# Windowed attention with sinks, then a capacity-limited expert layer: half values by DMA, wider masks, scores two steps ahead

## The chip, the cores and the metric

The kernel runs on one core of a Trainium2 chip. The metric is the device time of one execution in microseconds, lower is better. Its engines are named as in the profile: PE (TensorE matmuls, with PEld for the weight loads), DVE (VectorE), ACT (ScalarE), POOL (GpSimd) and SP (SyncE, which here only issues DMAs). Each engine takes its instructions in the order in which the program issued them.

## What is computed

Four batches of eight heads, 768 positions, 64 elements a head. Attention sees the last 128 positions and the first four ("sinks"):

```
scores = scale * q @ k.T
keep   = (pos_k < 4) | ((rel >= 0) & (rel < 128))
a      = softmax(where(keep, scores, -1e9));  x = a @ v     # heads side by side: x is (4, 768, 512)
```

Then, for each batch, the 128 rows of x with the highest x @ w_gate go through an expert and are written over:

```
h  = relu(x[top] @ w1);  ye = h @ w2
out[top] = x[top] + sigmoid(score) * ye            # all other rows: out = x
```

## The kernel before, in words

**Steps.** The loop (line 380) runs over 24 steps: batch b, head group g (four heads), and jp, a pair of 128-row blocks of queries. Within a batch the six steps are numbered s = 3g + jp. Every engine's order is the order of the calls in this loop (`manual_schedule`, line 59); waits between engines follow from the tiles they share.

**Scores (line 188).** For each of e = 0, 1 (two heads each) PE multiplies a block of 128 keys with up to 256 queries into a PSUM tile `sc`, then the four sink keys against the halves of the blocks that need them. ACT takes exp of each `sc` (line 214) into a tile `pt`, one for each e. The exps need no maximum, since the scores are small.

**Masks (lines 218 to 232).** POOL sets to zero what lies outside the window, in place in `pt`: for each e four selections, on 64 partitions each, of 256 elements (128 for a part of jp = 2, where the last block has no successor), and at jp = 0 a memset of the four sink rows, where the sinks are ordinary keys. That is eight selections a step.

**Values (line 234).** For each e PE multiplies the masked weights with values, 16 products (12 at jp = 0), each recorded as two matmul instructions, into a PSUM tile `xg`. A column of ones behind the 64 values gives the sum of the weights; DVE takes its reciprocal and scales (lines 253, 254) into the tile `X` of the batch. There are two `xg`. The products use the full values `vb`, or one of two half tiles: `vlo` has the values of the lower 64 keys of each block and the sink values in rows from 64 on, `vhi` the values of the upper 64 and the sink values in rows from 0 on. So a product of 128 rows covers 64 window keys and the sinks.

**Where the half values come from.** The rest of `vlo` and `vhi` is zero (memsets on DVE, lines 140 to 143). SP writes the four sink rows from a tile `vst` (line 113). POOL copies the halves from `vb` (line 118), 64x512 elements at a time, two copies in each step, three steps ahead of use: group 1 of a batch during its steps 0 to 2, group 0 of the next batch during steps 3 to 5; the first group in the head.

**Transposes (line 163).** Queries and keys come by POOL's DMAs (line 84) into `kb` and `qb`, and PE turns them in groups of twelve into PSUM tiles `trp`, of which there are two (tag "w"); ACT and DVE copy one half each into `KT` and `QT`. For the next head group, keys are turned at jp = 0 and queries at jp = 1. `sink_keys` copies the sink columns.

**Expert layer (class Moe).** It runs one batch behind, in pieces put into the steps: scores spread and counted (s = 0, 1), rank and selection matrix (s = 2), row indices (s = 3), a gather of the chosen rows by an indirect DMA on POOL (s = 4, line 329), their transposition and the first product (s = 5); the second product and the scatter on POOL (line 365) follow in steps 0 to 2 of the batch after. The last batch's layer is the tail behind the loop.

**Head.** POOL issues eight loads of the first q and k in halves, then makes the identity matrix for the transposes (line 131), which DVE casts (line 133). DVE then clears the half tiles. All transposes of the first group stand ahead of the first scores (lines 372 to 377), and each step's scores are issued one step ahead of its values (line 386).

Of the kernel before, what the change touches and what calls it, by code (L numbers as in the profile page):

```python
# [15 lines left out]
B = 4  # L16
# [9 lines left out]
VS = 96  # L26
# [4 lines left out]
def kernel(  # L31
# [19 lines left out]
    pp = ctx.enter_context(tc.tile_pool(name="pp", bufs=6))  # L51
# [9 lines left out]
    def const(shape, dt, name):  # L61
        return cp.tile(shape, dt, name=name, tag=name)

    vb = [const([128, H, NB, VS], FP32, f"vb{i}") for i in range(2)]
# [53 lines left out]
    def copy_half_values(b, g, c0, c1):  # L118
        for dst, r in ((vlo, 0), (vhi, 64)):
            POOL.tensor_copy(out=dst[g][r:r + 64, :, c0:c1, 0:D], in_=vb[b % 2][r:r + 64, 4 * g:4 * g + 4, c0:c1, 0:D])  # L120
# [6 lines left out]
    DVE.memset(ident_f[:], 0.0)  # L127
    DVE.memset(vb[0][:, :, :, D:VW], 1.0)
    DVE.memset(ksk[0][:], 0.0)
    DVE.memset(ksk[1][:], 0.0)  # L130
    POOL.affine_select(out=ident_f[:], in_=ident_f[:], compare_op=ALU.not_equal, fill=1.0, base=0,
                       pattern=[[-1, 128]], channel_multiplier=1)
    DVE.tensor_copy(out=ident_b[:], in_=ident_f[:])  # L133
    load_qk(0, 1)
    DVE.memset(vst[:, :, :, D:VW], 1.0)
    for g in range(2):
        ACTE.copy(out=vst[:, 4 * g:4 * g + 4, :, 0:D],
                  in_=vsk[:, 4 * g:4 * g + 4, :].unsqueeze(2).to_broadcast((NSINK * B, 4, NB, D)))
    for g in range(2):
        DVE.memset(vlo[g][64:128, :, :, :], 0.0)  # L140
# [3 lines left out]
        load_sink_values(0, g)  # L144
        if g == 0:
            for jp in range(3):
                copy_half_values(0, 0, 2 * jp, 2 * jp + 2)
# [40 lines left out]
    def scores(b, g, jp):  # L188
# [11 lines left out]
        for e in range(2):  # L200
            qh = qt[:, e, :].rearrange("p (c m n) -> p c m n", m=2, n=64)
            last = 1 if jp == 2 else 2
            for l in range(2):
# [5 lines left out]
                          start=True, stop=True, skip_group_check=True)  # L209
        for e in range(2):  # L210
            pt = pp.tile([128, 2, 2, 256], FP32, name="pt", tag="pt")
            PT[(b, g, jp, e)] = pt
            if jp < 2:
                ACTE.activation(out=pt[:, :, :, :], in_=sc[e][:, :, :, :], func=ACT.Exp, scale=0.125)  # L214
            else:
                ACTE.activation(out=pt[:, :, 0, :], in_=sc[e][:, :, 0, :], func=ACT.Exp, scale=0.125)
                ACTE.activation(out=pt[:, :, 1, 0:128], in_=sc[e][:, :, 1, 0:128], func=ACT.Exp, scale=0.125)
            for r in (0, 64):
                o = pt[r:r + 64, :, :, r:r + 64].rearrange("p l c n -> p (l c) n")
                POOL.affine_select(out=o, in_=o, compare_op=ALU.is_ge, fill=0.0,  # L220
                                   base=0, pattern=[[0, 4], [1, 64]], channel_multiplier=-1)
            for r in (0, 64):
                if jp < 2:
                    o = pt[r:r + 64, :, :, 128 + r:192 + r].rearrange("p l c n -> p (l c) n")
                    n = 4
                else:
                    o = pt[r:r + 64, :, 0, 128 + r:192 + r]
                    n = 2
                POOL.affine_select(out=o, in_=o, compare_op=ALU.is_ge, fill=0.0,  # L229
                                   base=-1, pattern=[[0, n], [-1, 64]], channel_multiplier=1)  # L230
            if jp == 0:
                POOL.memset(pt[0:NSINK, :, 0, :].rearrange("p l (w n) -> p l w n", w=2)[:, :, :, 0:64], 0.0)  # L232

    def values(b, g, jp, t):
        xg = x_ps.tile([128, 2, 2, VW], FP32, name="xg", tag="xg")
        full = vb[b % 2][:, 4 * g:4 * g + 4, :, :]
        for i in range(2):
            j = 2 * jp + i
            new = PT[(b, g, jp, t)]
            old, o = (PT[(b, g, jp, t)], 0) if i else (PT.get((b, g, jp - 1, t)), 1)  # L240
            for l in range(2):
                hh = 2 * l + t
                terms = []
                if j:
                    terms.append((old[:, l, o, 128:192], full[:, hh, j - 1, 0:VW], 0))
                    terms.append((old[:, l, o, 192:256], vhi[g][:, hh, j - 1, :], 1))
                terms.append((new[:, l, i, 0:64], vlo[g][:, hh, j, :], 0))
                terms.append((new[:, l, i, 64:128], full[:, hh, j, 0:VW], 1))
# [123 lines left out]
    for t in range(2):  # L372
        transposes(0, 0, t, (0,))
    for t in range(2):
        transposes(0, 0, t, (1,))
    sink_keys(0, 0)
    scores(0, 0, 0)

    moe = {}
    for n, (b, g, jp) in enumerate(steps):  # L380
# [24 lines left out]
        if nxt[0] < B and jp == 0:  # L405
            transposes(nxt[0], nxt[1], 0)
# [94 lines left out]
```

## Time and profile before

| | us |
|---|---|
| median of 3 runs | 207.34 (206.05 to 207.49) |
| the profiled execution | 206.85 |
| its span in the trace | 205.1 |

The span is what the trace covers; the rest of the execution's time lies around it. In the stage tables each row is a stretch of the span: its length, the busy time of each engine with its count of instructions, the clock that PE was granted, the mean share of the sixteen DMA engines and GB/s. A line of a group reads: line, engine, operation, tiles written and read, shape, count, then busy us and mean ns of one, then the idle time before such instructions and what ended it. A line of the waits reads: who waited for whom, us in total, times, longest.

Two things about the numbers. PE's busy time includes the drain at the end of each burst of matmuls, so it is more than the time in which PE issues. And DMA shares can exceed 1, since packets of several queues overlap.

### The profile page before, as it was taken

The numbers are of one execution on the slowest core, as the hardware profiler recorded it, in microseconds if no ns is written. First come the engines' busy times: TensorE is split into PE (matmuls) and PEld (weight loads), VectorE is DVE, ScalarE is ACT, GpSimd is POOL, SyncE is SP. The second block draws the span as 40 slices with busy tenths as digits, with TensorE's granted clock in tenths as the row PEclk, the third lists the DMA queues.
The fourth block names the chain that finished last, engine by engine and source line by source line (L and its number), as shares of the span: only waits on it lengthen the run. The fifth ranks groups of instructions, "written<-read, shape, count | busy, mean of one in ns | idle before, by whom it ended". The sixth has DMA issues, their size and how long they took to land. (4 is left out here: it accounts for less than half of the span.)

```text
span 205.1 us, 5901 instructions
## 1 busy us (share of the span) xinstructions
PE 134.0 (65%) x2476; PEld 108.3 (53%) x2480; DVE 95.2 (46%) x286; ACT 74.4 (36%) x108; POOL 141.3 (69%) x295
## 2 busy tenths in 40 slices
PE   0317887598488929952999670780699945949470
PEld 0303775585387717841797460660587734837440
DVE  0581374186437725670078650353049751572610
ACT  0805454163316331430474542030265543332030
POOL 7933898988989889883798880784778785800111
PEclk9999999769859985695599998596589985666996
DMA  5999927087392999948508149024000012240111
GB/s 83 219 178 216 288 46 136 5 137 225 114 275 51 198 190 195 232 173 261 152 0 148 21 74 234 4 105 158 6 3 3 3 52 105 104 153 3 51 51 53
DMA packets 21786, 24.14 MB, mean 118 GB/s; under 512 B 7232, under 2 KB 17472, under 8 KB 21760
## 3 DMA queue, kind: packets, MB, share of 16 engines
q0 software_dynamic: 7168, 10.49, 28.2%
q1 hardware_dynamic: 14592, 13.28, 22.0%
q8 instruction: 19, 0.31, 0.6%
q14 instruction: 7, 0.06, 0.1%
HBM read 24.41 MB, written 7.34 MB: 155 GB/s over the span
## 5 line engine op out<-in xcount | busy, mean ns | idle before, releaser
L250 PE MATMUL xg<-vb,pt 128*64 128x65 f32 x704 | 62.6, 254 | 10.5 <-POOL pt L220 9.4
L250 PE MATMUL xg<-vlo,pt 128*64 128x65 f32 x384 | 56.6, 255 | 17.5 <-POOL pt L232 15.6
L220 POOL TENSOR_SCALAR_AFFINE_SELECT pt<-pt 64x256 f32<-64x256 f32 x96 | 42.2, 440 | 29.1 <-DMA out_dram<-yo,idx 8.8
L250 PEld LDWEIGHTS xg<-vb,pt 128*64 128x64 f32 x704 | 54.1, 164 | 13.5 <-POOL pt L220 11.4
L250 PEld LDWEIGHTS xg<-vlo,pt 128*64 128x64 f32 x384 | 43.8, 165 | 20.3 <-POOL pt L232 17.8
L250 PE MATMUL xg<-vhi,pt 128*64 128x65 f32 x320 | 48.8, 251 | 0.6 <-POOL pt L229 0.4
L214 ACT ACTIVATE pt<-sc 128x1024 f32<-128x1024 f32 x32 | 31.0, 1021 | 38.8 <-PE sc L207 36.2
L229 POOL TENSOR_SCALAR_AFFINE_SELECT pt<-pt 64x256 f32<-64x256 f32 (+1 forms) x96 | 38.7, 403 | 6.0
L253 DVE RECIPROCAL rz<-xg 128x4 f32<-128x4 f32 x48 | 8.7, 182 | 67.6 <-PE xg L250 67.3
L250 PEld LDWEIGHTS xg<-vhi,pt 128*64 128x64 f32 x320 | 37.4, 162 | 2.5 <-POOL pt L229 2.4
L254 DVE TENSOR_TENSOR x<-xg,rz 128x256 f32<-128x256 f32 x48 | 20.4, 425 | 1.7
L294 DVE TENSOR_SCALAR_CACHE_REDUCE G<-sbc,scol 128x256 bf16<-128x256 f32 (+5 forms) x28 | 15.6, 608 | 8.1 <-ACT sbc L287 8.1
L264 DVE CUSTOM_DVE_ANT_0 junk<-x,wgb 128x512 f32<-128x512 f32 x24 | 17.7, 774 | 0.3
L197 PE MATMUL sc<-QT,KT 64*128 64x256 bf16 x192 | 16.5, 295 | 1.9 <-ACT pt L214 1.3
L120 POOL COPY vlo<-vb 64x512 f32<-64x512 f32 x24 | 14.6, 608 | 1.9 <-DMA vb<-in_v_dram 0.6
L120 POOL COPY vhi<-vb 64x512 f32<-64x512 f32 x24 | 14.8, 615 | 1.0
L366 POOL DMA_INDIRECT out_dram<-yo,idx x4 | 4.2, 1043 | 16.1 <-DVE rank L306 11.9
L173 PE MATMUL trp<-ident_b,kb 128*64 128x128 bf16 x192 | 9.5, 266 | 8.1 <-DVE ident_b L133 7.1
L181 ACT COPY KT<-trp 128x768 bf16<-128x768 bf16 x7 | 5.7, 809 | 21.1 <-PE trp L173 21.1
L173 PE MATMUL trp<-ident_b,qb 128*64 128x128 bf16 x192 | 9.5, 255 | 5.8 <-DVE KT L183 4.7
L353 PE MATMUL hps<-xeT,w_sb 128*128 128x128 bf16 x128 | 11.4, 265 | 2.7 <-ACT xeT L345 2.7
L173 PEld LDWEIGHTS <-kb 128*64 128x64 bf16 x192 | 8.4, 142 | 8.2 <-issue 8.2
(73 smaller groups left out, 194.2 us busy)
## 6 DMA issues: line engine op xcount, KB each, us to landing
out_dram<-x SPq DMA_DIRECT2D x12, 512.0 KB
kb<-in_k_dram POOLq DMA_DIRECT2D x7, 384.0 KB, 5.0
qb<-in_q_dram POOLq DMA_DIRECT2D x7, 384.0 KB, 8.4
w_sb<-in_moe_w_dram POOLq DMA_DIRECT2D x2, 1024.0 KB, 12.6
vb<-in_v_dram SPq DMA_DIRECT2D x6, 128.0 KB
vb<-in_v_dram SPq DMA_DIRECT2D x1, 768.0 KB
kb<-in_k_dram POOLq DMA_DIRECT2D x4, 96.0 KB, 4.1
qb<-in_q_dram POOLq DMA_DIRECT2D x4, 96.0 KB, 5.0
```

What stands on the lines that cost most here:

```text
L120: POOL.tensor_copy(out=dst[g][r:r + 64, :, c0:c1, 0:D], in_=vb[b % 2][r:r + 64, 4 * g:4 * g + 4, c0:c1, 0:D])
L173: PE.transpose(out=trp[64 * l:64 * l + 64, i, :], in_=src[:, l, half * (CT // 2) + i, :], identity=ident_b[:])
L197: PE.matmul(out=sc[e][:, l, r, 0:nq], lhsT=kt[64 * l:64 * l + 64, e, kc * 128:(kc + 1) * 128], rhs=qt[64 * l:64 * l + 64, e, kc * 128:kc * ...
L214: ACTE.activation(out=pt[:, :, :, :], in_=sc[e][:, :, :, :], func=ACT.Exp, scale=0.125)
L220: POOL.affine_select(out=o, in_=o, compare_op=ALU.is_ge, fill=0.0, base=0, pattern=[[0, 4], [1, 64]], channel_multiplier=-1)
L229: POOL.affine_select(out=o, in_=o, compare_op=ALU.is_ge, fill=0.0, base=-1, pattern=[[0, n], [-1, 64]], channel_multiplier=1)
L250: PE.matmul(out=xg[64 * m:64 * m + 64, i, l, :], lhsT=p, rhs=w, start=(i == 0 and l == 0 and n < 2), stop=(i == 1 and l == 1 and n >= len( ...
L253: DVE.reciprocal(out=rz[:, :, :, :], in_=xg[:, :, :, D:VW])
L254: DVE.tensor_tensor(out=X[b][:, 2 * jp:2 * jp + 2, 256 * g:256 * g + 256].rearrange("p j (l e d) -> p j l e d", l=2, e=2)[:, :, :, t, :], ...
L264: DVE.tensor_tensor_reduce(out=junk[:, :], in0=X[b][:, j, :], in1=wgb[:, :], scale=1.0, scalar=0.0, op0=ALU.mult, op1=ALU.add, accum_out=S ...
L294: DVE.tensor_scalar(out=self.G[c][:, a:hi], in0=self.sbc[:, a:hi], scalar1=SCOL[self.b][:, c:c + 1], scalar2=0.0, op0=ALU.is_gt, op1=ALU.a ...
L353: PE.matmul(out=hps[:, f, :], lhsT=w1_sb[:, dc, fc * 128:(fc + 1) * 128], rhs=self.xeT[:, dc, :], start=(dc == 0), stop=(dc == 3))
```

## The change

- POOL's copies of half values become transfers on SP's queue, one pair for a whole head group: group 1 of a batch after the values of its step 0, group 0 of the next batch after step 3, each behind the sink rows of the same tiles. For that `vb` loses its padding (`VS` = 96 becomes `VW` = 65), so that a row of `vb` is contiguous and holds the ones too.
- The very first half values come from HBM, block by block between the loads of `vb`, twelve DMAs of 64 partitions.
- The two tiles `pt` of a step become one, of twice the size, and each selection covers both e: four a step of 64x512 (two of them 64x256 at jp = 2). The pool has four tiles instead of six.
- Scores are issued two steps ahead, between the two halves of the values of a step.
- Keys and queries of the next group are turned in one step, after the values at jp = 0.
- In the head POOL makes the identity first, ahead of its loads; the first scores follow the first half of the transposes, and the second step's scores are ahead of the loop too.

```diff
-    def copy_half_values(b, g, c0, c1):
+    def copy_half_values(b, g):
         for dst, r in ((vlo, 0), (vhi, 64)):
-            POOL.tensor_copy(out=dst[g][r:r + 64, :, c0:c1, 0:D], in_=vb[b % 2][r:r + 64, 4 * g:4 * g + 4, c0:c1, 0:D])
+            SP.dma_start(out=dst[g][r:r + 64, :, :, :].rearrange("p h c d -> p (h c d)"),
+                         in_=vb[b % 2][r:r + 64, 4 * g:4 * g + 4, :, :].rearrange("p h c d -> p (h c d)"))
+
+    def load_half_values(c):
+        for m, dst in enumerate((vlo, vhi)):
+            r = 64 * m
+            SP.dma_start(out=dst[0][r:r + 64, :, c, 0:D],
+                         in_=v[0, 0:4, c * 128 + r:c * 128 + r + 64, :].rearrange("h p d -> p h d"))
+    POOL.memset(ident_f[:], 0.0)
+    POOL.affine_select(out=ident_f[:], in_=ident_f[:], compare_op=ALU.not_equal, fill=1.0, base=0,
+                       pattern=[[-1, 128]], channel_multiplier=1)
     load_qk_first()
...
     for c in range(NB):
         load_v_block(0, 0, c)
+        load_half_values(c)
+    DVE.memset(vst[:, :, :, D:VW], 1.0)
+    DVE.tensor_copy(out=ident_b[:], in_=ident_f[:])
     DVE.memset(vb[0][:, :, :, D:VW], 1.0)
...
+        pt = pp.tile([128, 2, 2, 2, 256], FP32, name="pt", tag="pt")
...
+        for r in (0, 64):
+            o = pt[r:r + 64, :, :, :, r:r + 64].rearrange("p e l c n -> p (e l c) n")
+            POOL.affine_select(out=o, in_=o, compare_op=ALU.is_ge, fill=0.0,
+                               base=0, pattern=[[0, 8], [1, 64]], channel_multiplier=-1)
...
-    for t in range(2):
-        transposes(0, 0, t, (0,))
-    for t in range(2):
-        transposes(0, 0, t, (1,))
-    sink_keys(0, 0)
-    scores(0, 0, 0)
+    for half in range(2):
+        for t in range(2):
+            transposes(0, 0, t, (half,))
+        if half == 0:
+            sink_keys(0, 0)
+            scores(0, 0, 0)
+    scores(0, 0, 1)
...
-        if n + 1 < len(steps):
-            nb, ng, njp = steps[n + 1]
-            scores(nb, ng, njp)
-        nb, ng = (b, 1) if s < 3 else (b + 1, 0)
-        if nb < B:
-            if jp == 0 and (nb, ng) != (0, 1):
-                load_sink_values(nb, ng)
-            copy_half_values(nb, ng, 2 * jp, 2 * jp + 2)
-        if nxt[0] < B:
-            if jp == 1:
-                transposes(nxt[0], nxt[1], 1)
-                sink_keys(*nxt)
         for t in range(2):
             values(b, g, jp, t)
+            if t == 0 and n + 2 < len(steps):
+                scores(*steps[n + 2])
...
-        if nxt[0] < B and jp == 0:
-            transposes(nxt[0], nxt[1], 0)
+        if jp == 0 and nxt[0] < B:
+            for t in range(2):
+                transposes(nxt[0], nxt[1], t)
+            sink_keys(*nxt)
+        if s == 0:
+            load_sink_values(b, 1)
+            copy_half_values(b, 1)
+        elif s == 3 and b + 1 < B:
+            load_sink_values(b + 1, 0)
+            copy_half_values(b + 1, 0)
```

More of the change, by code (lines that the diff above doesn't have):

```diff
@@ L126 @@
         load_v_block(0, 0, c)
-    DVE.memset(ident_f[:], 0.0)
+        load_half_values(c)
+    DVE.memset(vst[:, :, :, D:VW], 1.0)
+    DVE.tensor_copy(out=ident_b[:], in_=ident_f[:])
     DVE.memset(vb[0][:, :, :, D:VW], 1.0)
[L129 to L133, printed above, removed]
+    for i in range(2):
+        DVE.memset(ksk[i][:], 0.0)
     load_qk(0, 1)
[L135 to L138, printed above, removed]
     for g in range(2):
@@ L143 @@
         DVE.memset(vhi[g][64:128, :, :, D:VW], 1.0)
[L144 to L147, printed above, removed]
+        ACTE.copy(out=vst[:, 4 * g:4 * g + 4, :, 0:D],
+                  in_=vsk[:, 4 * g:4 * g + 4, :].unsqueeze(2).to_broadcast((NSINK * B, 4, NB, D)))
+    load_sink_values(0, 0)
     load_v(0, 1, 2)
@@ L222, in scores @@
[L222 to L232, printed above, removed]
+                ACTE.activation(out=pt[:, e, :, 0, :], in_=sc[e][:, :, 0, :], func=ACT.Exp, scale=0.125)
```

40 lines of the change are left out of this document (22 added, 18 removed).

## The prediction

> **What bounds the kernel now.** I read the page first, then the stages, the queue of GpSimd in order of time, the groups by form and the waits. The page shows no engine above 69%, so an average says little.
>
> ```profile
> span 205.1 us, 5901 instructions
> PE 134.0 (65%) x2476; PEld 108.3 (53%) x2480; DVE 95.2 (46%) x286; ACT 74.4 (36%) x108; POOL 141.3 (69%) x295
> ```
>
> The stages (columns: length, then busy time of PE, PEld, DVE, ACT, POOL, then clock, DMA share, GB/s) are cut where POOL takes up the first mask of batches 0 to 3; then the whole stretch from the first to the last value matmul, and the tail behind it.
>
> ```profile
> 18.65:52.92 34.27, 27.68 (x560) 22.01 (x559) 16.43 (x51) 14.90 (x21) 30.51 (x68) 0.90 0.62 138
> 52.92:92.31 39.39, 27.84 (x563) 23.57 (x555) 22.61 (x66) 14.91 (x22) 35.30 (x71) 0.78 0.85 185
> 20.86:179.90 159.04, 114.71 (x2267) 94.30 (x2269) 78.10 (x232) 61.33 (x92) 125.73 (x266) 0.81 0.51 119
> 179.90:205.10 25.20, 13.01 (x133) 9.93 (x131) 8.80 (x36) 5.04 (x9) 2.98 (x4) 0.80 0.18 63
> ```
>
> In batches 0 and 1 POOL is busy 30.51 of 34.27 and 35.30 of 39.39 us. Its queue in one step shows why: eight selections and two copies without a pause. The last two rows below are the one kind of pause: the selection behind an indirect DMA starts only when that has landed.
>
> ```profile
> 59.40 0.89 POOL L220 TENSOR_SCALAR_AFFINE_SELECT pt<-pt 64x256 f32<-64x256 f32 x2
> 60.35 0.89 POOL L229 TENSOR_SCALAR_AFFINE_SELECT pt<-pt 64x256 f32<-64x256 f32 x2
> 61.31 0.89 POOL L220 TENSOR_SCALAR_AFFINE_SELECT pt<-pt 64x256 f32<-64x256 f32 x2
> 62.26 0.89 POOL L229 TENSOR_SCALAR_AFFINE_SELECT pt<-pt 64x256 f32<-64x256 f32 x2
> 63.20 0.60 POOL L120 COPY vlo<-vb 64x512 f32<-64x512 f32 x1
> 63.85 0.61 POOL L120 COPY vhi<-vb 64x512 f32<-64x512 f32 x1
> 67.61 0.64 POOL L229 TENSOR_SCALAR_AFFINE_SELECT pt<-pt 64x128 f32<-64x128 f32 x2
> 120.84 1.19 POOL L366 DMA_INDIRECT out_dram<-yo,idx  x1 [0.30 <-issue]
> 129.20 0.41 POOL L220 TENSOR_SCALAR_AFFINE_SELECT pt<-pt 64x256 f32<-64x256 f32 x1 [6.71 <-DMA out_dram<-yo,idx]
> ```
>
> So the 159.04 us of the loop are POOL's: 125.73 busy, the rest landings and issue. PE, with 114.71, waits for masks:
>
> ```profile
> PE xg L250 <- POOL pt L232: 15.6, 11, 2.8
> PE xt L343 <- DMA xe<-out_dram,idx: 14.3, 3, 6.0
> PE xg L250 <- POOL pt L220: 10.5, 5, 6.8
> DVE idx L322 <- DMA out_dram<-yo,idx: 10.9, 3, 7.4
> ```
>
> **The change, POOL's part.** The loop's groups by form (mean ns behind the busy time):
>
> ```profile
> L220 POOL TENSOR_SCALAR_AFFINE_SELECT pt<-pt 64x256 f32<-64x256 f32 x96 | 42.2, 440 | 29.1 <-DMA out_dram<-yo,idx 8.8 <-ACT pt L214 8.4 <-DMA xe<-out_dram,idx 6.5
> L229 POOL TENSOR_SCALAR_AFFINE_SELECT pt<-pt 64x256 f32<-64x256 f32 x64 | 27.3, 426 | 3.9
> L120 POOL COPY vhi<-vb 64x512 f32<-64x512 f32 x24 | 14.8, 615 | 1.0
> L229 POOL TENSOR_SCALAR_AFFINE_SELECT pt<-pt 64x128 f32<-64x128 f32 x32 | 11.4, 357 | 2.1
> L232 POOL MEMSET pt<- 4x256 f32 x16 | 4.8, 301 | 0.9
> ```
>
> Copies: 42 of the 48 stand in the loop, 42 x 0.61 = 26 us gone. Selections: 192 cost 42.2 + 27.3 + 11.4 = 80.9 us. They become 80 of 64x512 and 16 of 64x256. No row has a 64x512 selection: below stands the copy of that size, 0.61 us, above two of half the size, 0.89. From 64x128 (0.64/2) to 64x256 (0.89/2) each 128 elements add 0.125, so I take 0.445 + 0.25 = 0.70, between the ends: 80 x 0.70 + 16 x 0.43 = 63 us, a gain of 18 (25 to 3 at the ends). Sixteen memsets become eight of twice the size, a gain of 1 to 2. POOL falls from 125.73 to about 80 us busy. With the waits behind indirect DMAs (8.8 + 6.5 us) and issue it needs about 105, up to 120 at the dear end. It stops being the bound, and PE's 114.71 comes forward.
>
> **Scores two steps ahead.** Values of step n need masks whose scores were issued one and a half steps earlier. At the price of two exps (1.94 us below) and four selections with a memset (3.3) that chain is 5.3 us against about 8.6 us of lead at 138/24 = 5.75 us a step. The masks are hidden except behind a scatter. The price: one tile now holds both e, so POOL starts only after both exps and the first values after all four selections; this costs the head about a microsecond, counted there. Four tiles of twice the size cover n-1 to n+2, no wait.
>
> **Half values by SyncE.** In the loop seven pairs of 400 KB. The copies stand ahead of the next batch's load of values; at the half of a batch they stand behind that load, which must land first. Queued behind them on SP are the stores of x, for which only a gather some four steps later waits. Nearest rows of that size:
>
> ```profile
> kb<-in_k_dram POOLq DMA_DIRECT2D x7, 384.0 KB, 5.0
> qb<-in_q_dram POOLq DMA_DIRECT2D x7, 384.0 KB, 8.4
> w_sb<-in_moe_w_dram POOLq DMA_DIRECT2D x2, 1024.0 KB, 12.6
> ```
>
> A pair should land 5 to 13 us after its issue; it has three steps, 17 us. Hidden, at nothing; without that cover each microsecond late costs one. Their 5.6 MB take 30 us of DMA at batch 1's 185 GB/s, 47 at the loop's mean of 119, beside 0.51 x 159 = 81 us in the loop: room, except in batch 1 (share 0.85). The head also loads 0.8 MB more from HBM.
>
> **Transposes, both in one step.** They share two PSUM buffers. The third group of twelve waits until ACT, busy with the two exps of the scores just issued (1.94 us below), has copied the first group (0.80 below). PE has value matmuls and two groups to do meanwhile, so the wait lies between nothing and 2.74 us; I take the middle, 1.4, seven times in the loop, 10 us. Bounds 0 and 19.
>
> **The head.**
>
> ```profile
> 1.38 1.46 POOL L100 DMA_DIRECT2D kb<-in_k_dram  x2 [0.84 <-POOLq L482]
> 6.52 0.29 POOL L131 TENSOR_SCALAR_AFFINE_SELECT ident_f<-ident_f 128x128 f32<-128x128 f32 x1
> 6.84 0.23 DVE L133 CAST ident_b<-ident_f 128x128 bf16<-128x128 f32 x1 [5.54 <-POOL ident_f L131]
> 7.51 1.36 DVE L140 MEMSET vlo<- 64x1560 f32 x1 [0.36 <-issue]
> 8.98 0.80 ACT L181 COPY QT<-trp 128x768 bf16<-128x768 bf16 x1
> 14.42 0.95 DVE L183 COPY KT<-trp 128x768 bf16<-128x768 bf16 x1
> 16.21 1.03 PE L197 MATMUL sc<-QT,KT 64*128 64x256 bf16 x8
> 17.55 1.94 ACT L214 ACTIVATE pt<-sc 128x1024 f32<-128x1024 f32 x2 [0.44 <-PE sc L207]
> 20.86 0.37 PE L250 MATMUL xg<-vlo,pt 128*64 128x65 f32 x1 [0.36 <-POOL pt L232]
> ```
>
> Now the cast of the identity sits on DVE until 6.84 and the memsets behind it hold the KT copy until 14.42. Early, the identity is ready near 2 us; the memsets (7.51 to 14.4, 6.9 us) end near 9.4. KT is there at 10.4, QT about then too (8.98 + 0.8 and a microsecond for later loads), since POOL's loads start some 0.6 us later and share DMA with 0.8 MB. Scores at 10.6 need only the first half; exps 1.34 us on (16.21 to 17.55), done near 13.9; masks 3.3: first values at 17.3 instead of 20.86, 3.5 us earlier. Bounds: 16 to 20, by when the loads land.
>
> **The clock.** Seven stretches of the loop ran at half the granted clock; first, last and their sum:
>
> ```profile
> 38.00:45.00 7.00, 5.88 (x104) 5.18 (x106) 4.07 (x10) 2.78 (x6) 6.39 (x13) 0.51 0.46 60
> 167.80:178.00 10.20, 7.17 (x100) 6.09 (x98) 3.71 (x15) 3.85 (x8) 7.19 (x16) 0.50 0.21 80
> sum 61.60, PE 42.62 PEld 36.93 DVE 18.26 ACT 16.25 POOL 43.92; mean PE 6.09 PEld 5.28 DVE 2.61 ACT 2.32 POOL 6.27
> ```
>
> At full clock their 42.62 us of PE would be about half, 21 less. With fewer mask waits I expect half of that, 10; ends 0 and 21. The Trainium skill (TensorE: Matmul & The Clock Gate, "Why this matters for your kernels") says that PE idle for more than about 3 us between bursts falls back to half clock and that it should stay full otherwise. By that rule and with no such gap left the sum below would be 11 us lower, 169 instead of 180; the trace agrees in so far as POOL waits of 6.71 us lie in half-clock stretches, but 38 to 45 has PE busy 5.88 of 7 and stays at 0.51.
>
> **The sum.** Loop: PE 114.7 - 10 = 104.7. Gathers: two of the three waits lie in the loop (12 us); the gather is now issued nearer to the step that needs it, about 3 us each, 6. Scatter before the index on DVE: 7.4 and about 2 remain, 9. Transposes 10. DVE behind the counts and row sums delays the release of xg, my estimate from 78.10 us of DVE in the loop: 3 us in each of three batches, 9. Together 138.7 instead of 159.0. Tail 25.2 as before: its chain of count, index, up and down is not touched. 17.3 + 138.7 + 25.2 = 181.2 us of span against 205.1. The profiled run took 206.85, so 1.75 lie around the span, and it stands 0.5 under the median of 207.34. That gives 183; PE busy counts the drains of short bursts that fuse when the waits go, for which I take off 3: 180.
>
> **Rivals.** (a) Full clock through the loop, 11 us less: 169. For it: the mask waits go. Against: gather and scatter still stop PE. (b) PE's waits all hide and POOL at 105 sets the loop: 17.3 + 105 + 25.2 + 1.75 = 149. Against: PE alone is 94 at full clock and has its own waits. (c) Batch 1 becomes bound by DMA: 0.85 x 39.39 = 33.5 us of DMA plus two pairs at 4.3 to 6.8 is 42 to 47 us in a batch that I give 33; some 10 us more with what the queues delay elsewhere: 190. (d) On the other side: the half copies land late. Seven pairs must each land 27/7 = 4 us after their need, 21 us after issue, for 207; the worst row above is 12.6 for 1 MB. For it: they move SBUF to SBUF, for which no large row exists. (e) The selection for the identity needs its code first, and that is ready only when this trace has the selection start, 6.52. Then POOL's loads, behind it, begin at 6.5 instead of 1.38, and 5 us of the head are lost: 185. The GPSIMD Engine Reference of the Trainium skill ("Instruction dispatch") states about 6 us for the first call after such a code load, by which it would be 186. The trace shows no such wait behind the load itself:
>
> ```profile
> L131 POOLq MODIFY_POOL_CONFIG  x2: 162/162/162, 6.3 to 6.3; - x2
> ```
>
> The selection followed within 0.3 us. That was at 6 us though, not at 1.
>
> **Numbers.** Forecast 0.52, (a) 0.20, (b) 0.04, (c) 0.14, (d) 0.06, (e) 0.04. 180 us; its own range 173 to 187. 162 to 194 leaves out (b), (d) and part of (c) and (a). Within 1% is about what a measurement can tell from no change; it needs most of (c) and (d) in part: 0.02. Faster 0.93, slower 0.05.
>
> **What would show it.** POOL under 105 us, no L120, selections of 64x512 near 0.70 us; first value matmul near 17.3; PE waits on POOL under 10 us; PE waits on trp copies near 10; clock above 0.81. Wrong if vlo or vhi from DMA stands among PE's waits, if POOL stays dense, or if PE stays at half clock.

## The result and the profile after

The changed kernel takes 201.46 us (median of four runs, 198.81 to 203.39) against 206.69 (205.88 to 207.49); the ratio is 0.956, its 95% interval 0.944 to 0.969. Medians and ranges here take in every run, while a ratio compares only the runs within 1.5% of the fastest of their kernel (for the change 198.81 and a fifth run of 196.47, 197.6 on average), and where one run alone is that fast no ratio is given. The forecast was 180, its range 162 to 194: the direction was right, the size was not, and the time lies outside the range either way. The trace is of a run of 203.17, near the upper end; it is read for where the waits are, not for a microsecond more or less, and how long the gather took in the run of 196.47 is not known.

The head of the page after, with its slices of POOL and of the DMA engines (tenths of a slice of 5 us):

```profile
span 201.5 us, 5765 instructions
PE 126.3 (63%) x2476; PEld 102.2 (51%) x2480; DVE 95.9 (48%) x285; ACT 74.7 (37%) x108; POOL 95.2 (47%) x144
POOL 8528074947776967300315666086330685101101
DMA  4999989999899999999923649823800021511101
```

POOL has fallen from 141.3 to 95.2 us, as the change meant it to, and its slices have holes. The DMA engines are at eight tenths or more from 5 to 100 us. The stages of after (length, then PE, PEld, DVE, ACT, POOL, clock, DMA share, GB/s): the loop from the first value matmul to the last, the tail, and 79 to 101 us:

```profile
21.15:173.88 152.73, 103.38 (x2267) 85.17 (x2269) 79.37 (x235) 60.31 (x90) 79.30 (x116) 0.87 0.75 170
173.88:201.50 27.62, 17.02 (x133) 13.11 (x131) 8.16 (x32) 4.94 (x9) 2.95 (x3) 0.62 0.14 48
79.00:101.00 22.00, 2.73 (x20) 2.45 (x20) 1.72 (x4) 0.72 (x2) 5.02 (x7) 0.57 1.10 249
```

In the last row all engines nearly stand still, PE busy 2.73 of 22 us, and the DMA engines are full. The first reciprocal of a step on DVE, when half of its values are done, serves as the step's mark. The expert layer of batch 0 takes up its gathered rows between the marks of steps 11 and 12; first before, then after:

```profile
88.61 0.17 DVE L253 RECIPROCAL rz<-xg 128x4 f32<-128x4 f32 x1
102.49 0.18 DVE L253 RECIPROCAL rz<-xg 128x4 f32<-128x4 f32 x1 [10.54 <-PE xg L250]
```

```profile
77.55 0.17 DVE L256 RECIPROCAL rz<-xg 128x4 f32<-128x4 f32 x1
102.80 0.18 DVE L256 RECIPROCAL rz<-xg 128x4 f32<-128x4 f32 x1 [22.08 <-PE xg L253]
```

At step 11 after was 11 us ahead (77.55 against 88.61). At step 12 it was level (102.80 against 102.49): this stretch takes 25.2 us instead of 13.9. The second half (step 12 to 23) then takes 69.2 instead of 75.95 us, and the tail gives some of that back. POOL's rows for the place, first the gather before, then after, and PE's row after:

```profile
90.79 1.47 POOL L331 DMA_INDIRECT xe<-out_dram,idx  x1 [0.28 <-POOL vhi L120]
```

```profile
80.29 1.33 POOL L334 DMA_INDIRECT xe<-out_dram,idx  x1 [0.17 <-POOL pt L235]
81.67 0.65 POOL L223 TENSOR_SCALAR_AFFINE_SELECT pt<-pt 64x512 f32<-64x512 f32 x1
97.61 0.66 POOL L223 TENSOR_SCALAR_AFFINE_SELECT pt<-pt 64x512 f32<-64x512 f32 x1 [15.29 <-DMA xe<-out_dram,idx]
```

```profile
97.60 1.12 PE L346 MATMUL xt<-ident_f,xe 128*128 128x128 f32 x4 [19.39 <-DMA xe<-out_dram,idx]
```

The gather (256 KB) is issued at 80.29, ten us earlier than before (90.79), and lands at 97.6, later than before (95.9). PE's wait of 19.39 us begins at 78.21, two us ahead of the issue. How long the four gathers took to land, before and after, and then the page's issues of after (KB each, us to landing):

```profile
DMA to landing us min/median/max: 3.3/4.2/5.1
```

```profile
DMA to landing us min/median/max: 3.5/3.8/17.3
```

```profile
vlo<-vb SPq DMA_DIRECT2D x7, 390.0 KB, 8.0
vhi<-vb SPq DMA_DIRECT2D x7, 390.0 KB, 10.1
kb<-in_k_dram POOLq DMA_DIRECT2D x7, 384.0 KB, 8.0
w_sb<-in_moe_w_dram POOLq DMA_DIRECT2D x2, 1024.0 KB, 19.8
```

The half values land in 8 and 10 us in the median, inside their bounds (single ones in 5.3 to 14.9). But the loads of keys have gone from 5.0 to 8.0 us and those of the expert's weights from 12.6 to 19.8. The gather stands in POOL's DMA queue behind such loads. The last of them, the queries of batch 2's second head group, was issued ten us ahead of the gather:

```profile
70.27 0.72 POOL L88 DMA_DIRECT2D qb<-in_q_dram  x1
```

```profile
DMA to landing us min/median/max: 26.2/26.2/26.2
```

It lands 26.2 us after its issue, at 96.5, and the gather 1.1 us behind it. Before, the load in that place had landed, at 89.0, when the gather was issued.

PE's waits in the loop of after (us in total, times, longest):

```profile
PE xt L346 <- DMA xe<-out_dram,idx: 23.0, 2, 19.4
PE xg L253 <- DVE rz L256: 10.4, 3, 7.0
PE trp L176 <- ACT KT L184: 3.6, 5, 1.0
PE xg L253 <- issue: 2.9, 3, 1.1
PE xg L253 <- POOL pt L235: 2.6, 3, 1.9
PE xg L253 <- POOL pt L232: 0.7, 1, 0.7
PE xg L253 <- DMA vhi<-vb: 0.2, 1, 0.2
```

PE's waits for POOL's masks, 26.5 us before, are down to 3.3. The gathers are up from 12.0 (in the loop) to 23.0. And the head, whose first values were to come at 17.3:

```profile
1.54 1.47 POOL L99 DMA_DIRECT2D kb<-in_k_dram  x2
9.15 0.95 DVE L186 COPY KT<-trp 128x768 bf16<-128x768 bf16 x1
14.93 1.37 POOL L232 TENSOR_SCALAR_AFFINE_SELECT pt<-pt 64x512 f32<-64x512 f32 x2
16.35 0.52 POOL L235 MEMSET pt<- 4x512 f32 x1
18.32 0.71 SPq L114 DMA_DIRECT2D vlo<-vst  x1
21.15 0.34 PE L253 MATMUL xg<-vlo,pt 128*64 128x65 f32 x1 [5.57 <-DMA vlo<-vst]
```

The masks were ready at 16.9, but the sink rows of `vlo` stood on SP behind eighteen block loads, and were issued at 18.32. So PE began at 21.15, later than before.

**The theory, and its rivals.** Theory one, the queue: the transfers (and the head's extra loads) keep the DMA engines full until 100 us, and the gather of batch 0, behind the weights and the next loads on POOL's queue, lands when that backlog is worked off, however early it is issued. Theory two, the place: with scores two steps ahead, the gather comes behind more masks on POOL and is issued too near to its use. Theory three: the head's late sink rows. A fourth: POOL's relief is worth less than its busy time says. The runs went in four groups. Their expectations call theory one Q (or T, where the total of the transfers counts) and theory two P; S is that POOL bounds the kernel before, R and R2 are rivals of the run they stand in.

### The profile page after: what moved, and what is told of

Its sections match the earlier page's. It is cut to its first block, busy times and chain, and to the rows that moved or that the text cites. A ratio compares the mean times of both kernels' runs of the same rounds, so it can differ in the third digit from the quotient of the medians.

```text
span 201.5 us, 5765 instructions
## 1 busy us (share of the span) xinstructions
PE 126.3 (63%) x2476; PEld 102.2 (51%) x2480; DVE 95.9 (48%) x285; ACT 74.7 (37%) x108; POOL 95.2 (47%) x144
## 5 line engine op out<-in xcount | busy, mean ns | idle before, releaser
L223 POOL TENSOR_SCALAR_AFFINE_SELECT pt<-pt 64x512 f32<-64x512 f32 x48 | 36.4, 758 | 74.1 <-ACT pt L217 28.4
L253 PE MATMUL xg<-vb,pt 128*64 128x65 f32 x704 | 58.2, 239 | 12.6 <-DVE rz L256 10.4
L253 PEld LDWEIGHTS xg<-vb,pt 128*64 128x64 f32 x704 | 50.5, 150 | 16.7 <-issue 13.6
L253 PE MATMUL xg<-vlo,pt 128*64 128x65 f32 x384 | 51.4, 239 | 9.1 <-DMA vlo<-vst 5.6
L253 PEld LDWEIGHTS xg<-vlo,pt 128*64 128x64 f32 x384 | 40.2, 151 | 11.1 <-POOL pt L232 5.8
L253 PE MATMUL xg<-vhi,pt 128*64 128x65 f32 x320 | 45.0, 239 | 1.1 <-POOL pt L232 0.7
L253 PEld LDWEIGHTS xg<-vhi,pt 128*64 128x64 f32 x320 | 34.0, 149 | 1.5 <-POOL pt L232 0.9
L232 POOL TENSOR_SCALAR_AFFINE_SELECT pt<-pt 64x512 f32<-64x512 f32 (+1 forms) x48 | 28.6, 595 | 3.0
L219 ACT ACTIVATE pt<-sc 128x512 f32<-128x512 f32 x16 | 9.6, 601 | 20.7 <-PE sc L210 20.7
L356 PEld LDWEIGHTS <-w_sb 128*128 128x128 bf16 x128 | 12.4, 134 | 3.9 <-issue 3.9
L346 PEld LDWEIGHTS xt<-ident_f,xe 128*128 128x128 f32 x12 | 2.1, 217 | 23.9 <-DMA xe<-out_dram,idx 23.9
## 6 DMA issues: line engine op xcount, KB each, us to landing
vhi<-vb SPq DMA_DIRECT2D x7, 390.0 KB, 10.1
w_sb<-in_moe_w_dram POOLq DMA_DIRECT2D x2, 1024.0 KB, 19.8
```

The costliest lines, as they stand in the source:

```text
L219: ACTE.activation(out=pt[:, e, :, 0, :], in_=sc[e][:, :, 0, :], func=ACT.Exp, scale=0.125)
L253: PE.matmul(out=xg[64 * m:64 * m + 64, i, l, :], lhsT=p, rhs=w, start=(i == 0 and l == 0 and n < 2), stop=(i == 1 and l == 1 and n >= len( ...
L356: PE.matmul(out=hps[:, f, :], lhsT=w1_sb[:, dc, fc * 128:(fc + 1) * 128], rhs=self.xeT[:, dc, :], start=(dc == 0), stop=(dc == 3))
```

## Experiments: what each part does alone

**e4: only the new head in the kernel before.** The identity first, DVE's casts and memsets in the changed order, the first scores behind half of the transposes.

```diff
+    POOL.memset(ident_f[:], 0.0)
+    POOL.affine_select(out=ident_f[:], ...)
     load_qk_first()
...
+    DVE.tensor_copy(out=ident_b[:], in_=ident_f[:])
...
-    for t in range(2):
-        transposes(0, 0, t, (0,))
-    for t in range(2):
-        transposes(0, 0, t, (1,))
-    sink_keys(0, 0)
-    scores(0, 0, 0)
+    for half in range(2):
+        for t in range(2):
+            transposes(0, 0, t, (half,))
+        if half == 0:
+            sink_keys(0, 0)
+            scores(0, 0, 0)
```

> The kernel before, with the head's order alone: identity first on POOL, the casts and memsets of DVE in the changed order, the first scores behind the first half of the transposes. Half values by POOL, narrow masks, scores one step ahead as before. The prediction's step on the head: KT near 9.4 instead of 14.4, first values near 16 us instead of 20.9; POOL then bounds the loop from 14 us on, and the time falls by 4 to 5 us. If the loads bound the first steps, it falls by less than 2 us.

Measured 202.52 (202.0 to 202.88), ratio 0.976 (0.972 to 0.980). The first values come at 15.58 and the whole 5.3 us reach the end. With the copies on POOL, and so no added block loads on SP ahead of the sink rows, the head is worth what it saves.

**e11: only the wide masks in the kernel before.** One `pt` for both e, four selections a step, three tiles instead of six.

```diff
+        pt = pp.tile([128, 2, 2, 2, 256], FP32, name="pt", tag="pt")
...
-            pt = pp.tile([128, 2, 2, 256], FP32, name="pt", tag="pt")
...
```

> The kernel before with the wide masks alone: one tile for both e, four selections a step, scores one step ahead, half values copied by POOL. The prediction's price of a 64x512 selection, 0.70 us, makes 18 us less on POOL. Measured in the changed kernel: 0.68 alone. Theory S (POOL bounds the kernel before through and through): the time falls by 12 to 18 us. Rival (with one step of lead the masks now start only after both exps, and the wait for them takes the gain): by 0 to 6 us.

Measured 194.31 (191.33 to 194.96; before 206.76 on the same chip), 12.5 us less. Its page:

```profile
PE 128.2 (66%) x2480; PEld 105.1 (54%) x2480; DVE 98.1 (51%) x286; ACT 74.5 (39%) x108; POOL 125.0 (65%) x191
```

POOL is busy 16 us less than before, and three quarters of that come out at the end. So POOL did bound the loop, the fourth theory fails, and the smaller half of POOL's relief alone beats the whole change: every run of e11 is below every run of the change.

**e12: only the transfers, in the loop of the kernel before.** No edit of masks, scores or head; `vb` loses its padding, as in the change.

```diff
-    vb = [const([128, H, NB, VS], FP32, f"vb{i}") for i in range(2)]
+    vb = [const([128, H, NB, VW], FP32, f"vb{i}") for i in range(2)]
...
+    def dma_half_values(b, g):
+        for dst, r in ((vlo, 0), (vhi, 64)):
+            SP.dma_start(out=dst[g][r:r + 64, :, :, :]..., in_=vb[b % 2][r:r + 64, 4 * g:4 * g + 4, :, :]...)
...
-            copy_half_values(nb, ng, 2 * jp, 2 * jp + 2)
+                dma_half_values(nb, ng)
```

> The kernel before with the loop's half values moved by SP in pairs, all else as before, narrow masks and one step of lead. POOL loses 42 copies, 26 us. If POOL bounds the kernel through and through, and the transfers are hidden: the time falls by 18 to 26 us. Theory Q: POOL gets faster and meets the loads' queue at the gather of batch 0, which leaves earlier and lands no earlier than about 90 us; the time falls by 8 to 15 us, most of it in the second half.

Measured 197.42 (195.89 to 203.36), ratio 0.949 (0.943 to 0.955): faster, since 26 us of copies leave POOL. But its step 11 to 12 takes 20.7 us where before had 13.9. The gather is issued at 76.66, and PE's waits and the landing show why:

```profile
PE xt L348 <- DMA xe<-out_dram,idx: 18.6, 3, 13.2
```

```profile
DMA to landing us min/median/max: 3.2/3.5/13.6
```

The transfers alone, without the two steps of lead, stretch the gather's landing from 5.1 to 13.6 us. That the gather also leaves 14 us earlier is not the reason: the next run's leaves as early, at 76.01, behind the same loads but without transfers, and lands in 3.7 us.

**e13: head and wide masks together in the kernel before.** The edits of e4 and e11.

> The kernel before with the changed head and the wide masks, half values by POOL, one step of lead: no added traffic in the loop. Alone the head gave 5.3 us and the masks 12.5. If the two add: 188 to 190 us. If the loads of the first half take the head's gain, as in the changed kernel: 193 to 196 us.

Measured 188.44 (185.14 to 189.9; before 207.02): 18.6 us less, where e4 and e11 sum to 17.8. These two parts add. By the medians the three parts alone gave 5.3, 12.5 and 9.3, together 27; the change, which has all three, gave 5 (9 by the ratio). So some 20 us are lost where they meet, or to what none of the three has: the two steps of lead, the transposes in one step and the head's half values from HBM.

## Experiments: the queue ahead of the gather

**e1: the changed kernel, sink rows behind the first two blocks.**

```diff
-    for c in range(NB):
+    for c in range(2):
         load_v_block(0, 0, c)
         load_half_values(c)
...
     load_sink_values(0, 0)
+    for c in range(2, NB):
+        load_v_block(0, 0, c)
+        load_half_values(c)
```

> The changed kernel, with the sink rows of the first half tiles issued on SP behind the loads of blocks 0 and 1 instead of behind all eighteen block loads. In the changed kernel's trace the masks of step 0 end at 16.9 us and the first values start near 22.5, PE waiting 5.6 us for the sink rows. Theory T (the transfers fill the DMA engines until about 100 us, and that sets the first half): the first values start 5 us earlier, but the gather of batch 0's expert layer lands no more than 2 us earlier than 97 us, and the time falls by 0 to 2 us. Rival R (the head's delay passes through to the end): the time falls by 4 to 6 us.

Measured 202.44 (198.61 to 208.63), no gain against 201.46. The head did come right:

```profile
16.95 0.37 PE L256 MATMUL xg<-vlo,pt 128*64 128x65 f32 x1 [1.34 <-POOL pt L238]
```

That is four us earlier than 21.15 (not 22.5, as the expectation has it), and close to the 17.3 of the prediction. The mark of step 0 comes at 18.56 instead of 23.33, but that of step 12 at 104.52 instead of 102.80: the gather, issued at 84.5, landed 14.8 us later, again one us behind the load of queries ahead of it (98.3). The head's four us are real and are lost at the gather, so theory three explains the 21.15 and not the 201.

**e3: the changed kernel, w2 loaded four steps later.**

```diff
-        if n == 7:
+        if n == 11:
             POOL.dma_start(out=w2_sb...
```

> The changed kernel, with the load of the second expert matrix (1 MB in bf16, POOL's DMA queue) four steps later, behind the gather in that queue. Theory Q (the gather waits in POOL's DMA queue behind the loads issued before it): PE's wait for the gather falls from 19 us to 5 to 10 us, and the time falls by 5 to 9 us. If it is only the engines' total work up to 100 us that counts, the wait falls by less and the time by less than 3 us.

Measured 194.81 (193.15 to 197.76), ratio 0.936 (0.930 to 0.942), against 0.956 for the change: about four us, where five to nine were expected. One load of 1 MB moved out from ahead of the gather: PE's waits for gathers fall to 14.9 us, the longest to 9.8, the worst landing from 17.3 to 8.1, and step 12 has its mark at 96.94. The queue is the cause of a good part.

**e7: e1 and e3 together.**

> The changed kernel with two moves: sink rows behind blocks 0 and 1 on SP, and the second weight matrix behind the gather. With the weight alone the median was 194.8 us, with the sink rows alone 202.4, no different from the changed kernel. Theory Q: the head's gain still runs into the queue, less so than before: 191 to 195 us. If the head's gain passes through once the backlog is shorter: 188 to 191 us.

Measured 196.91 (192.83 to 199.78), ratio 0.934 (0.926 to 0.942), so no more than e3 alone. Step 12 has its mark at 94.99, two us earlier than in e3, but then w2 itself is late:

```profile
PE ye L366 <- DMA w_sb<-in_moe_w_dram: 5.0, 1, 5.0
```

**e5 and e6: the changed kernel and the kernel before, both without the two weight loads.** The weights are a constant from small memsets in the first steps.

```diff
-        if n == 6:
-            POOL.dma_start(out=w1_sb...
-        if n == 7:
-            POOL.dma_start(out=w2_sb...
+        if n in (2, 3, 4, 5):
+            DVE.memset(w1_sb[:, n - 2, :], 0.01)
+            DVE.memset(w2_sb[:, 2 * n - 4:2 * n - 2, :], 0.01)
```

> The changed kernel without the two loads of expert weights (4 MB read from HBM); a constant is written to the weight tiles instead, so the expert rows are wrong. Theory Q (the gather of batch 0 waits behind the backlog of POOL's DMA queue, of which the weights are 12 us): the gather lands 3.5 to 6 us after its issue instead of 17, PE's longest wait for it falls from 19.4 to 3 to 8 us, and the time falls by 9 to 14 us. If the gather were slow by itself, or by the half-value transfers on the other queue, the wait stays over 12 us and the time falls by less than 4.

> The kernel before without the two loads of expert weights, as a control: its gather was issued at 90.8 us, late because POOL was late, and landed in 5.1 us. Theory Q: POOL sets that kernel's time and the queue is nearly drained by then, so the time falls by 0 to 3 us. If the weights' traffic cost both kernels alike, it falls as much as in the changed one.

e6, the control: 208.24, ratio 1.002 (0.999 to 1.005). In the kernel before the weights cost nothing. e5: 195.69 (191.65 to 197.59), some 6 us below 201.46, not the 9 to 14 expected. With 2 MB less (as written to the tiles) ahead of it the gather lands in 8.4 us and PE still waits 15.0 us for gathers, the longest 10.5. So the loads ahead are a cause but not all: PE's long wait, which ends at 91.3, began at 80.8, and the gather was only issued at 82.9. That spoke for theory two.

**e2: the changed kernel, half values copied by POOL again in the loop.**

```diff
-            SP.dma_start(out=dst[g][r:r + 64, :, :, :]..., in_=vb[b % 2][...])
+            POOL.tensor_copy(out=dst[g][r:r + 64, :, c0:c1, 0:D], in_=vb[b % 2][...])
```

> The changed kernel, with the half values in the loop copied by POOL again, two copies of 64x512 a step behind the masks, and no transfers on SP for them; wide masks, order and head as changed. POOL gets 42 x 0.65 = 27 us back, on 95 busy. Theory T: the DMA engines lose 7 pairs (about 22 us of their time), the gather that landed near 97 us lands 8 to 15 us earlier, and the time falls by 6 to 12 us in spite of POOL's work. Rival R2 (the transfers cost nothing, POOL's work does): the time rises by up to 10 us.

Measured 199.22 (198.38 to 200.54), ratio 0.961 (0.956 to 0.966). Without the transfers the landing falls from 17.3 to 8.6 us, but POOL, with 120.6 us busy, issues the gather only at 85.4; PE's longest wait for it stays at 13.8. It was expected to gain 6 to 12 us and gained nothing that can be told from noise (0.956 for the change): the later issue on POOL took what the queue gave.

**e8: e7 and e2 together.**

> As the run with both moves, and the half values in the loop copied by POOL again instead of transfers. Traffic is least here. Theory Q: the gather lands within 6 us and the time is 186 to 192 us, POOL having room for 27 us of copies. If POOL's copies delay masks and gather as much as the traffic did: 193 to 198 us.

Measured 197.24 (196.77 to 198.26), ratio 0.950 (0.946 to 0.954). Transfers gone, w2 late, the head right, and still 21.2 us of PE's waits for gathers, the longest 13.2. The backlog of POOL's queue alone cannot be the answer: the load of queries ahead of the gather had landed at 77.7, the gather was issued only at 81.64, and it still took 9.3 us to land. Just ahead of it, at 80.80, SP had issued the load of a whole batch's values; that these two shared the DMA engines is likely the reason, but no run tests it.

## Experiments: the place of gather and scatter

**e14: the changed kernel with scores one step ahead again.**

```diff
+        if n + 1 < len(steps):
+            scores(*steps[n + 1])
         for t in range(2):
             values(b, g, jp, t)
-            if t == 0 and n + 2 < len(steps):
-                scores(*steps[n + 2])
```

> The changed kernel with scores issued one step ahead, at the start of a step, as before; transfers, masks and head as changed. Theory P (two steps of lead put the gather and scatter behind masks that are scored later): the time falls by 2 to 8 us against the changed kernel's 201. If the lead pays (the prediction), the time rises by 3 to 8 us. If the traffic alone takes the gains, it stays within 2 us.

Measured 196.0 (193.93 to 196.72), ratio 0.945 (0.939 to 0.952); this interval and that of the change (0.944 to 0.969) overlap, so that less lead is faster is not shown, but the forecast that more lead pays is not borne out either. PE's waits for gathers fall to 11.5 us, the longest 8.7, and step 11 to 12 takes 16.1 us; PE's waits for masks rise from 3.3 to 18.5 us, so the lead does hide the masks.

**e9: the changed kernel, gather at the beginning of s = 4, scatter at the beginning of s = 2.** Both go ahead of that step's values, and so ahead of the masks of two steps on.

```diff
         last = b == B - 1
+        if m and s == 4:
+            m.gather()
+        if mm and s == 2:
+            mm.scatter()
         for t in range(2):
             values(b, g, jp, t)
...
-            elif s == 4:
-                m.gather()
...
-            elif s == 2:
-                mm.scatter()
```

> The changed kernel with the gather and the scatter issued at the start of their steps on POOL, ahead of the masks of the step two ahead, instead of behind them. Nothing else is moved. Theory P (with scores two ahead, the gather stands behind masks that PE's own step has yet to start, so it leaves about when PE already waits for it): in batch 2, where the DMA engines are idle, the step that picks the rows falls from 11.7 us to 5 to 8; in batch 1, where the queue of loads is full, by less; PE's waits for the gather fall from 23 us to 10 to 17 and the time by 5 to 10 us. If the place in POOL's order doesn't matter, under 2 us.

Measured 192.23 (186.64 to 193.57), every run below the fastest of the change (196.47). Its first gather is the plainest evidence for the queue:

```profile
74.57 1.04 POOL L334 DMA_INDIRECT xe<-out_dram,idx  x1 [2.27 <-issue]
76.86 0.65 POOL L223 TENSOR_SCALAR_AFFINE_SELECT pt<-pt 64x512 f32<-64x512 f32 x1 [1.24 <-ACT pt L217]
98.55 0.66 POOL L223 TENSOR_SCALAR_AFFINE_SELECT pt<-pt 64x512 f32<-64x512 f32 x1 [21.04 <-DMA xe<-out_dram,idx]
```

```profile
DMA to landing us min/median/max: 3.4/5.8/23.9
```

Issued 5.7 us earlier than in the change, it lands no earlier, at 98.5 for 97.6 (the wait behind it ends at 98.55, there at 97.61), and again 1.1 us behind the load of queries ahead of it (97.4). The run's gain comes from elsewhere: step 15 to 16, which computes the row indices of batch 1, takes 6.4 instead of 13.6 us, since DVE's index no longer waits 7.4 us for the scatter of batch 0. That scatter is issued 5.7 us earlier, at 116.65, and lands in 4.4 us instead of 8.8; in the change, at 122.37, it stood right behind two loads of keys and queries issued from 120.65 on, which it now precedes. Step 17 to 18, with the next gather, stays as it was (12.0 for 11.7): issued ten us earlier, at 127.19, it follows two loads of keys and queries issued from 123.11 on, in the same queue. So at the first gather theory one holds; at the scatter the place on POOL counts, in part because it sets what stands ahead in the queue.

**e17: e9 with the copies on POOL.**

> The changed kernel with two edits alone: half values in the loop by POOL, and gather and scatter at the start of their steps; the sink rows and the second weight matrix stay where the change has them. Each edit alone gave 199.2 and 192.2 us against 201.5; with both and the two further moves it was 180.6. If the traffic and the place of the gather are the cause between them: 181 to 186 us, the rest of the way being the sink rows and the weights. If the two further moves are needed for it: 188 to 192 us.

Measured 187.01 (185.68 to 187.34; before 207.3), ratio 0.898 (0.890 to 0.906). PE's waits for gathers are 14.0 us, the longest 9.1. Against e2, the same without the earlier gather and scatter, it is 12 us faster, and the intervals are far apart (0.956 to 0.966 there): this shows that the place of the two costs time.

## Experiments: all mended

**e10: sinks early, w2 late, gather and scatter early, transfers kept** (the edits of e1, e3 and e9).

> All moves together: sink rows early, second weight matrix behind the gather, gather and scatter at the start of their steps; transfers on SP kept. Theories Q and P add up: 184 to 190 us, with PE's longest wait for the gather under 5 us. If the loads' total until 100 us sets the first half whatever the order: 191 to 196 us.

Measured 188.35 (185.11 to 191.97), ratio 0.900 (0.892 to 0.909). PE waits 9.2 us for gathers, the longest 4.5, but now also 4.1 us for half values that land late, and 5.8 for w2.

**e15: e13 with w2 late.**

> As head and wide masks alone, with the second weight matrix behind the gather. Theory Q: with less traffic the queue in front of the gather is nearly empty, so the move gives 0 to 3 us here where it gave 6.7 in the changed kernel.

Measured 190.93 (187.53 to 192.01), ratio 0.913 (0.903 to 0.922), against 188.44 for e13. Without transfers and lead the weights stand in nobody's way, and moving them brings nothing.

**e16: as e10, but with the half values copied by POOL.** From the change there remain the wide masks, two steps of lead, the transposes and the new head with its half values from HBM.

> The changed kernel with sink rows early, second weight matrix late, gather and scatter at the start of their steps, and half values by POOL: against 188.4 us with transfers. If the transfers' traffic still costs when the order is mended: 184 to 187 us. If POOL's 27 us of copies cost as much behind the gather's landing: 188 to 193 us.

Measured 180.64 (180.1 to 182.8), ratio 0.875 (0.868 to 0.881): the best version, 26 us below the kernel before and 21 below the change (17 by the ratios). Its page, the loop's stage, and the place of the first gather:

```profile
PE 123.5 (69%) x2476; PEld 99.4 (56%) x2480; DVE 95.9 (54%) x285; ACT 74.7 (42%) x108; POOL 120.3 (67%) x186
```

```profile
16.90:154.00 137.10, 104.31 (x2243) 85.38 (x2247) 78.22 (x231) 60.71 (x91) 107.08 (x162) 0.89 0.69 149
```

```profile
77.62 1.54 POOL L336 DMA_INDIRECT xe<-out_dram,idx  x1 [0.28 <-POOL vhi L119]
79.20 0.65 POOL L225 TENSOR_SCALAR_AFFINE_SELECT pt<-pt 64x512 f32<-64x512 f32 x1
82.22 0.66 POOL L225 TENSOR_SCALAR_AFFINE_SELECT pt<-pt 64x512 f32<-64x512 f32 x1 [2.36 <-DMA xe<-out_dram,idx]
```

```profile
PE xg L255 <- POOL pt L237: 6.3, 3, 3.9
PE xt L348 <- DMA xe<-out_dram,idx: 5.9, 2, 3.8
PE trp L178 <- ACT KT L186: 5.6, 7, 1.0
PE ye L365 <- DMA w_sb<-in_moe_w_dram: 3.4, 1, 3.4
```

No gather takes more than 4.5 us to land, and step 11 to 12 takes 8.0 us instead of 25.2. POOL is busier than in the change by 25 us, and the kernel is faster. The mends need each other: e8 has all of e16 but the early gather and scatter (197.24, so these bring 16.6 there), e17 all but the sinks and w2 (187.01, so these bring 6.4), e10 has the transfers instead of the copies (188.35, so the transfers cost 7.7, or 5 by the ratios). Part of what the earlier gather brings against e8 is again the queues: it leaves at 77.62, ahead of SP's load of values (83.19), and lands in 4.5 us instead of 9.3.

## Why the prediction was wrong

**Hidden transfers (wrong, the first failed step).** "Half values by SyncE ... Hidden, at nothing" looked at who waits for the half values. That part held: PE waits 0.2 us for `vhi` from `vb`. What failed was the other side, what the 5.6 MB do to the transfers that share the DMA engines with them. The working set their 30 to 47 us of DMA time beside the 81 us in which the engines were already busy in the loop of 159 us, found room, and set batch 1 aside as an exception. Batch 1 is where the weights load and where the first gather has to pass: its landing went from 5.1 to 17.3 us, and to 13.6 with the transfers alone (e12), against 3.7 at the same time without them (e13). Rival (c) named the right place and gave it ten us; it had the whole batch bound by the sum of DMA work, and not one gather behind loads in a queue.

**Gathers at 3 us each (wrong, the second).** I took 6 us for two; the loop has 23.0. The reason that I gave, "issued nearer to the step that needs it", was no reason for a shorter wait. The scores of step n+2 now stand ahead of the gather, and I did not count their masks as work that it queues behind on POOL. e17 against e2, and e16 against e8, show this place; e3, e9 and e12 show the queue. e16, with both mended, shows 5.9 us, about the 6 I wrote.

**First values at 17.3 (21.15; wrong, but not what decided).** The chain was right in each of its steps but one: DVE's KT copy begins at 9.15 (forecast 9.4), the masks are ready at 16.9. Left out were the sink rows, behind twelve added DMAs on SP. That queue was in the diff.

**The sum.** Head 21.15 for 17.3, loop 152.73 for 138.7, tail 27.62 for 25.2: 20.3 us over. In the loop PE's busy time was right (103.38 for 104.7, at a clock of 0.87 for 0.81). The gathers are 17.0 over; the scatter ahead of the index, seen as PE's wait for DVE, 10.4 for 9; the wait for `trp` copies 3.6 for 10, the middle of two bounds where the lower end was nearer; DVE's backlog after the counts, an estimate of 9, is hardly to be seen (two of PE's three waits for DVE, 9.9 of the 10.4, are for the scatter). Small waits that I gave no term add about 12 (of these the masks 3.3). The 3 us taken off for fused drains had no row, and nothing shows them. So two terms 15 us too dear hid part of those that were too cheap. That e16 lands on 180.64, with a loop of 137.10, is likewise in part luck: it still pays for POOL's copies, and its masks make PE wait longer (8.6 us) than the change's.

**What was right.** POOL's price: two 64x512 selections without a wait take 1.37 us, 0.68 each, and the mean of all 80 is 0.72 (forecast 0.70); POOL is busy 79.30 us in the loop (forecast about 80). POOL as the bound of the loop before (e11). That more lead hides the masks (3.3 us of waits, 18.5 in e14). That rival (e) would not come about: the selection for the identity starts at 1.10 us, and POOL's loads begin at 1.54 us instead of 1.38. The wait of about 6 us that the Trainium skill states for the first call after a code load (GPSIMD Engine Reference, "Instruction dispatch") is not to be seen here. The clock's rule (the Trainium skill, TensorE: Matmul & The Clock Gate, "Why this matters for your kernels") agrees where PE stood still, 0.57 between 79 and 101. The tail is a place where it does not: PE's longest wait from 173.88 on is 2.2 us, below the 3 that the Trainium skill gives there, and yet the clock falls from full to half between 184 and 186 and stays there with PE busy 7.05 of 8 us.

```profile
182.00:184.00 2.00, 1.10 (x18) 0.69 (x16) 2.00 (x11) 0.00 (x0) 0.00 (x0) 1.00 0.00 0
186.00:188.00 2.00, 2.00 (x22) 2.00 (x20) 0.38 (x3) 0.06 (x1) 0.05 (x1) 0.50 0.18 70
190.00:192.00 2.00, 2.00 (x21) 2.00 (x20) 0.00 (x0) 0.60 (x1) 0.00 (x0) 0.50 0.25 94
```

**What stays open.** In all these kernels the second selection behind an indirect DMA waits until that has landed (15.29 us in the change); a program without this wait was not tried. Why some versions vary more between runs (185.11 to 191.97 in e10, 180.1 to 182.8 in e16) was not settled; it is not the transfers alone, since e15, without them, goes from 187.53 to 192.01. Nor was it separated how much of the backlog is the seven pairs and how much the head's extra loads; e12, without those, has a landing of 13.6 of the 17.3 us. And no run moves SP's load of a batch's values, which stands beside the gather of e8.

## What to carry to other kernels

Work moved from an engine to the DMA engines is not free where its own reader can wait: ask which transfers share the engines with it, in the stage where the queues are full, and above all whether a gather on the critical path shares a queue with prefetches. When scores, loads or masks are moved further ahead, look for the small late instruction (a gather, a scatter, a row of sinks) that they now pass on its engine, and move it ahead too. And try the parts of a change alone: here each gained, by the medians 27 us in sum, and together they gained 5.

## What the hardware showed that was not expected

An indirect gather of 256 KB that took 3.5 us in a quiet queue took 17.3 in the change and 23.9 when issued 5.7 us earlier (e9): in both it landed 1.1 us behind the load queued ahead of it, so that load fixed its end, and not its own issue. Copies from SBUF to SBUF of 390 KB took 8.0 and 10.1 us, as long as or longer than the loads of keys, 384 KB from HBM, in the same kernel (8.0), and those took 5.0 before. And PE stayed at a clock of 0.50 through eight us of the tail in which it was busy for seven.
